# Idle products on the four quarters of the TensorE array in a kernel of linear attention and a mixture of experts

## The chip, the cores and the metric

The kernel runs on one core of one Trainium2 chip, in one launch. The metric is the device time of that launch in microseconds (us). Three runs before the change took 336.48, 336.76 and 333.15 us, median 336.48. PE is TensorE, PEld its loads of stationary operands, DVE is VectorE, ACT is ScalarE, POOL is GpSimd and SP is SyncE, which here only issues DMAs.

## The reference

A linear attention with 8 batches, 8 heads, 576 tokens and 64 columns feeds a soft mixture of 8 experts with 4 slots each. Cut to what is computed:

```
phi(x): p = x @ w_phi; p -= max|p| over the features; [exp(p), exp(-p)]      # 64 -> 2 x 128
kv = phi(k)^T v;  z = sum phi(k);  x = phi(q) kv / (phi(q) z + 1e-6)         # per batch and head
logits = x @ moe_phi                                                        # 4608 x 32 slots
d = softmax over tokens;  slots = d^T x                                     # 32 x 512
h = relu(slots @ w1[e]);  y = h @ w2[e]                                     # per expert, 512 -> 1024 -> 512
out = softmax over slots (logits) @ y                                       # 4608 x 512
```

## The kernel before

**Main loop.** The 64 pairs of batch and head are taken as 32 units of 1152 tokens. For each bank of four tiles of 128 tokens, `proj` (line 266) multiplies k and q by `w_phi` on the two halves of the array's rows, DVE takes maxima (lines 271 and 328), ACT takes exponentials (lines 297, 300, 333, 336), POOL weighs the values (line 286), and PE forms `kv` (`kvmm`, line 313, tile `kvp`) and the numerators (`num`, line 366, tile `psn`). Work of the mixture that can be done early (transposes `psx`, logits `psl`, slot sums `pss`) is put between.

**Close of the loop.** The last tokens' logits and the softmax over all tokens are finished (lines 514 to 616), in a chain of small steps between PE, DVE and ACT.

**The experts.** `layer1` (line 835, tile `hp`) and `layer2` (line 910, tile `yp`) multiply 32 columns at a time: four experts, or four chunks of the hidden layer, are put on the four quarters of the array's columns (`hp[...][32 * e:32 * e + 32]`, and `yp[q][g:g + 32]` with `g = 32 * (c % 4)`). Layer 2 runs in four quarters `q` of the output columns. When one is done, `slots` and `slots2` (lines 917 and 921, tiles `yt` and `psy`) sum it, and `outputs` (line 930, tile `pso`) multiplies the softmax over slots by it. DVE and ACT copy the result to `o` (line 934), and SP writes it out (line 935). The string `TAIL` sets the order of these steps.

**Weights.** The 64 tiles of the experts' weights (512 KB each, line 237) are read by SP in the second half of the kernel, as the buffers of the main loop are closed.

**Order.** The order of the main loop and of its close is written out in the string `ORDER`, one letter for each task. The tasks run on their engines in that order, and PE's whole program is one straight list of instructions without loops.

**Idle products.** `spin` (line 190) multiplies a 128 x 128 bf16 block by 512 columns, into a PSUM tile `psw` that nothing reads. It keeps PE at work while it would wait for others. There are 19 of these: `NWARM = 8` at the very start, while the first inputs come in; `NSPIN = 8` (letter `e`), six after the first two banks and one each after two of the first pieces of `kvmm`; and `NFIN = 3` (task `zspin`, letter `W`) in the close of the loop. In the program each is one load and one product.

A product of fp32 operands in the source stands in the trace as two loads and two products of its shape, and the counts below are those of the trace.

## Time and profile before

| | before |
|---|---|
| runs | 336.48, 336.76, 333.15 us |
| the profiled execution's own time | 332.36 us |
| its span, first to last instruction | 330.6 us |
| PE busy | 317.3 us (96%), 7094 products |
| PE's loads busy | 270.6 us (82%), 7094 loads |
| DVE, ACT, POOL busy | 239.7, 229.0, 160.9 us |
| read and written | 63.60 and 9.44 MB, 221 GB/s over the span |
| packets on the instruction queue of PE (q8) | 56, 0.92 MB |

The page names each group of instructions by line, engine, operation and tiles. The chain of waits follows the work that ended last back from the end: a piece named "issue" is time in which the engine at the end of the chain waited for nothing that the profile shows. A window is a stretch of the span, with each engine's busy time and, as xN, the instructions that ran in it, those included that were still running at its start. Two of the DMA queues, q8 and q14, carry instructions and not data.

### The profile page before, as it was taken

What the parts mean: (1) busy time and instruction counts of PE and PEld (TensorE: products, weight loads), DVE (VectorE), ACT (ScalarE), POOL (GpSimd) and SP (SyncE); (2) the same over time, 40 slices, a digit from 0 to 9 for tenths busy, and PEclk for the clock granted to TensorE, in tenths of its full rate; (3) what the DMA queues carried; (4) which work ended last, traced back from release to release, by engine and by line L of the source; (5) the groups of instructions that cost most, each with busy time, mean ns of one, the idle gap of its engine ahead of it and who ended that gap; (6) DMA issues with size and microseconds to landing.
All of it is one profiled execution on the core that took longest, in us unless ns stands there. A gap on an engine that the chain in (4) does not pass through costs nothing.

```text
span 330.6 us, 16700 instructions
## 1 busy us (share of the span) xinstructions
PE 317.3 (96%) x7094; PEld 270.6 (82%) x7094; DVE 239.7 (73%) x688; ACT 229.0 (69%) x674; POOL 160.9 (49%) x339
## 2 busy tenths in 40 slices
PE   8999999999999999999999999999999999998990
PEld 4899999999979999998799999987989864375640
DVE  1678888786879888778898877688869667423461
ACT  4899889878886997788688987867878361002450
POOL 2455676773547668642867687236767210200000
PEclk9999999999999999999999999999999999999996
DMA  7556376644755774574567846216533999997897
GB/s 253 163 162 206 107 230 216 227 175 125 283 169 171 237 279 189 172 234 130 162 205 239 288 146 227 95 36 239 171 109 97 378 404 342 412 410 288 322 392 279
DMA packets 23130, 74.12 MB, mean 224 GB/s; under 512 B 2576, under 2 KB 2960, under 8 KB 23056
## 3 DMA queue, kind: packets, MB, share of 16 engines
q1 hardware_dynamic: 22768, 72.65, 62.7%
q8 instruction: 56, 0.92, 1.1%
q10 hardware_dynamic: 288, 0.40, 0.4%
q14 instruction: 18, 0.15, 0.1%
HBM read 63.60 MB, written 9.44 MB: 221 GB/s over the span
## 4 chain that ended last, share of the span: by engine, by line
PE 88%; DVE 3%; issue 3%; POOL 2%; DMA 1%; ACT 0%; DVEq 0%; POOLq 0%; SPq 0%; ACTq 0%
PE kvp L313 22%; PE psn L366 20%; PE psk L266 11%; PE psq L266 11%; PE psx L719 5%; PE hp L835 4%; PE yp L910 4%; PE psl L423 3%; PE pso L930 2%; PE psw L190 2%; PE pss L455 1%; POOL vs L286 1%; DMA out<-o 1%; PE psd L448 1%; PE pss L570 1%
## 5 line engine op out<-in xcount | busy, mean ns | idle before, releaser
L286 POOL TENSOR_TENSOR vs<-vt,mk 128x520 f32<-128x520 f32 (+3 forms) x128 | 91.4, 730 | 64.2 <-ACT mk L275 45.5
L313 PE MATMUL kvp<-vs,kf 128*64 128x65 f32 (+1 forms) x2304 | 91.5, 229 | 0.4 <-POOL vs L286 0.3
L313 PEld LDWEIGHTS kvp<-vs,kf 128*64 128x64 f32 x2304 | 81.0, 138 | 6.7 <-POOL vs L286 1.8
L366 PE MATMUL psn<-kvs,qf 128*64 128x65 f32 x2304 | 79.9, 223 | 0.4 <-DVE un L382 0.3
L266 PE MATMUL psk<-wd,xs 64*128 64x128 f32 x576 | 76.3, 280 | 0.9 <-issue 0.7
L366 PEld LDWEIGHTS psn<-kvs,qf 128*64 128x64 f32 x2304 | 73.4, 138 | 3.4 <-issue 0.7
L266 PE MATMUL psq<-xs,wd 64*128 64x128 f32 x576 | 75.5, 280 | 0.0
L266 PEld LDWEIGHTS psk<-wd,xs 64*128 64x128 f32 x576 | 67.7, 187 | 4.2 <-issue 2.5
L266 PEld LDWEIGHTS psq<-xs,wd 64*128 64x128 f32 x576 | 67.3, 187 | 3.4 <-issue 1.1
L271 DVE TENSOR_REDUCE mk<-psk 128x4 f32<-128x512 f32 x72 | 48.5, 675 | 11.6 <-PE psk L266 6.7
L328 DVE TRANSPOSE_TENSOR_REDUCE mts<-psq 128x16 f32<-128x512 f32 x72 | 50.4, 705 | 8.1 <-PE psk L266 3.3
L297 ACT ACTIVATE kf<-psk 128x512 f32<-128x512 f32 x72 | 42.5, 591 | 16.7 <-DVE mk L271 5.1
L333 ACT ACTIVATE qf<-psq 128x512 f32<-128x512 f32 x72 | 42.2, 594 | 10.2 <-DVE dn L397 3.7
L412 POOL TENSOR_TENSOR xc<-un,dn 128x256 f32<-128x256 f32 x62 | 37.9, 614 | 17.5 <-DVE dn L397 14.3
L377 DVE TENSOR_TENSOR un<-psn,eq 128x195 f32<-128x195 f32 x96 | 33.0, 351 | 16.3 <-PE psn L366 7.7
L336 ACT ACTIVATE qf<-psq 128x512 f32<-128x512 f32 x72 | 43.0, 601 | 0.8 <-DVE mts L328 0.8
L300 ACT ACTIVATE kf<-psk 128x512 f32<-128x512 f32 x72 | 42.7, 596 | 0.1
L382 DVE TENSOR_TENSOR un<-psn,un 128x195 f32<-128x195 f32 x96 | 32.9, 350 | 1.1
L344 ACT ACTIVATE mh<-mts 32x36 f32<-32x36 f32 x128 | 29.5, 230 | 3.2 <-DVE mts L328 1.6
L350 DVE TENSOR_REDUCE eq<-mh 32x9 f32<-32x36 f32 x128 | 26.3, 205 | 1.5
L274 ACT ACTIVATE mk<-mk 128x4 f32<-128x4 f32 x72 | 15.1, 209 | 11.2 <-DVE mk L271 9.9
L934 DVE COPY o<-pso 128x384 f32<-128x384 f32 x24 | 12.1, 551 | 14.2 <-PE pso L930 14.2
(121 smaller groups left out, 313.3 us busy)
## 6 DMA issues: line engine op xcount, KB each, us to landing
wt<-w SPq DMA_DIRECT2D x64, 512.0 KB, 5.9
xs<-xT SPq DMA_DIRECT2D x36, 512.0 KB, 4.3
vt<-vv SPq DMA_DIRECT2D x31, 325.0 KB, 3.8
out<-o SPq DMA_DIRECT2D x24, 384.0 KB, 4.2
vt<-vv ACTq DMA_DIRECT2D x1, 325.0 KB, 3.5
xs<-xT SPq DMA_DIRECT2D x2, 128.0 KB, 3.3
cs<-cst SPq DMA_DIRECT2D x1, 128.0 KB, 3.0
wd<-w ACTq DMA_DIRECT2D x1, 64.0 KB, 1.8
```

Source lines behind the costliest of these rows:

```text
L266: nc.tensor.matmul(ps, l, r, start=True, stop=True)
L271: nc.vector.tensor_reduce(km[b][:, 2], kx[b], axis=AX, op=ALU.max, apply_absolute_value=True)
L286: nc.gpsimd.tensor_tensor(vs[b][:, :, place(b, u, t, o):place(b, u, t, o) + n], v[:, t + o:t + o + n].unsqueeze(1).broadcast_to([128, 2, n ...
L297: nc.scalar.activation(kf[b][:, 1], kx[b], AF.Exp, scale=-1.0)
L300: nc.scalar.activation(kf[b][:, 0], kx[b], AF.Exp)
L313: nc.tensor.matmul(ps[f:f + FE // 2, pn, o:o + m], kf[b][:, pn, NT * u + t - 4 * b, f:f + FE // 2], v2[:, pn, at:at + m], start=(t == 0 an ...
L328: nc.vector.tensor_reduce(mts.rearrange("p r j -> p j r")[:, o:o + 4], qx[b].rearrange("p j (r t) -> p (j r) t", t=32), axis=AX, op=ALU.ma ...
L333: nc.scalar.activation(qf[b][:, 0], qx[b], AF.Exp)
L336: nc.scalar.activation(qf[b][:, 1], qx[b], AF.Exp, scale=-1.0)
L366: nc.tensor.matmul(ps[64 * f:64 * f + 64, j, pn], q2[:, pn, 64 * f:64 * f + 64], kv[:, pn, b2], start=True, stop=True)
L377: nc.vector.tensor_tensor(un[u][:, CH * c:CH * c + CH], nx[s][:, :, 0], e[:, 1].unsqueeze(2).broadcast_to([128, CH, 65]), op=ALU.mult)
L412: divider(u).tensor_tensor(x[:, :, h * D:(h + 1) * D], un[u][:, a:b, 0:64], dn[u][:, a:b].unsqueeze(2).broadcast_to([128, b - a, 64]), op= ...
```

## The change

A second function, `spins`, does an idle product as eight: the four quarters of 32 columns of the same block, each by 256 columns, and this twice, into the two halves of the same PSUM tile. All thirteen idle products from the last two of the first eight on use it: two of `NWARM`, all eight of `NSPIN`, all three of `NFIN`. The first six stay as they were. Each of the thirteen is now 16 instructions and not 2, so PE's program is 13 x 14 = 182 instructions longer: 28 of these stand before the first `proj`, 84 in the six idle products after the first two banks, 28 in the two among the first pieces of `kvmm`, and 42 in the close of the loop. All 182 stand ahead of layer 1 and layer 2. No wait, no DMA and no other instruction is added, on PE or elsewhere, and nothing else changes its place.

```diff
     def spin(ps, x):
         nc.tensor.matmul(ps.rearrange("p (a c) -> p a c", c=128), x, x.unsqueeze(1).broadcast_to([128, 4, 128]), start=True, stop=True)
+
+    def spins(ps, x):
+        for j in range(8):
+            g = slice(32 * (j % 4), 32 * (j % 4) + 32)
+            nc.tensor.matmul(ps[g, 256 * (j // 4):256 * (j // 4) + 256].rearrange("p (a c) -> p a c", c=128), x[:, g], x.unsqueeze(1).broadcast_to([128, 2, 128]), start=True, stop=True)
+
     for i in range(NWARM):
-        spin(pmm.tile([128, 512], F32, tag="mm", name="psw"), warm)
+        (spin if i < NWARM - 2 else spins)(pmm.tile([128, 512], F32, tag="mm", name="psw"), warm)
...
-        add("spin", i, PE, 0.22 if i > 1 else 0.43, lambda: spin(bank3("spin", [128, 512], "psw"), warm), after=[("proj", 0)], get=["psn", ("nm", "spin")], put=["psn", ("nm", "spin")], lat=0.0, at=1e6)
+        add("spin", i, PE, 0.22 if i > 1 else 0.43, lambda: spins(bank3("spin", [128, 512], "psw"), warm), after=[("proj", 0)], get=["psn", ("nm", "spin")], put=["psn", ("nm", "spin")], lat=0.0, at=1e6)
...
-        add("zspin", i, PE, 0.22, lambda: spin(bank3("spin", [128, 512], "psw"), cs[:, 0:64].bitcast(mybir.dt.bfloat16)), at=1e6, after=[("num", NK - 1)], get=["psn", ("nm", "spin")], put=["psn", ("nm", "spin")], lat=0.0)
+        add("zspin", i, PE, 0.22, lambda: spins(bank3("spin", [128, 512], "psw"), cs[:, 0:64].bitcast(mybir.dt.bfloat16)), at=1e6, after=[("num", NK - 1)], get=["psn", ("nm", "spin")], put=["psn", ("nm", "spin")], lat=0.0)
```

PE's list in the close of the loop before, around the first of the three idle products there (`psl` are logits, `psd` a transpose, `cs` holds the identity):

```order
L531 MATMUL psl<-xT,phs 32x128 x4
L531 MATMUL psl<-xm,phs 32x128
L190 LDWEIGHTS cs
L190 MATMUL psw<-cs 128x512
L423 MATMUL psl<-xT,phs 32x128 x12
L448 MATMUL psd<-cs,eT 128x128
```

The same place now, from the same first row, cut after the fourth of the eight loads and products:

```order
L537 MATMUL psl<-xT,phs 32x128 x4
L537 MATMUL psl<-xm,phs 32x128
L195 LDWEIGHTS cs
L195 MATMUL psw<-cs 32x256
L195 LDWEIGHTS cs
L195 MATMUL psw<-cs 32x256
L195 LDWEIGHTS cs
L195 MATMUL psw<-cs 32x256
L195 LDWEIGHTS cs
L195 MATMUL psw<-cs 32x256
```

Four more such pairs follow, and then the logits as before: one load and one product became eight of each, and the neighbours stay.

PE's list in layer 2 before, from the sum of the first quarter on (each x4 of `yp` is eight products in the trace):

```order
L921 MATMUL psy<-yt,cs 128x128
L910 MATMUL yp<-wt_5808,sh 32x128 x4
L910 MATMUL yp<-wt_5925,sh 32x128 x4
L930 MATMUL pso<-ct,yt 128x384 x4
L910 MATMUL yp<-wt_5927,sh 32x128 x4
L910 MATMUL yp<-wt_5929,sh 32x128 x4
```

The same place now:

```order
L927 MATMUL psy<-yt,cs 128x128
L916 MATMUL yp<-wt_5878,sh 32x128 x4
L916 MATMUL yp<-wt_5995,sh 32x128 x4
L936 MATMUL pso<-ct,yt 128x384 x4
L916 MATMUL yp<-wt_5997,sh 32x128 x4
L916 MATMUL yp<-wt_5999,sh 32x128 x4
```

Here nothing moved but line and buffer numbers: each instruction stands 182 places further down in PE's program than before.

## The prediction

> **What bounds the kernel now.** I read the page first, then the waits of PE, then the chain of waits around the largest of them.

> ```profile
> PE 317.3 (96%) x7094; PEld 270.6 (82%) x7094; DVE 239.7 (73%) x688; ACT 229.0 (69%) x674; POOL 160.9 (49%) x339
> q8 instruction: 56, 0.92, 1.1%
> PE 88%; DVE 3%; issue 3%; POOL 2%; DMA 1%; ACT 0%; DVEq 0%; POOLq 0%; SPq 0%; ACTq 0%
> PE yp L910 <- issue: 1.4, 1, 1.4
> PE psk L266 <- issue: 0.7, 1, 0.7
> ```

> PE is busy 96% of the span and carries 88% of the chain, so what is put on PE's path, or taken off it, moves the end nearly one for one. Its largest waits in mid-kernel, 1.4 and 0.7 us, are for "issue": no engine and no data transfer released them. The queue q8 holds 56 packets, one for every 14,188 / 56 = 253 of PE's products and loads. So I read it as the queue that brings PE's own instructions, a block at a time. Here is the chain of waits in layers 1 and 2 (start, us, what):

> ```profile
> 287.52 3.57 PE hp L835 x32
> 291.09 1.31 PE yp L910 x48
> 292.40 1.02 PE psh L888 x8
> 293.42 3.63 PE yp L910 x128
> 297.05 0.42 PE psy L921 x2
> 297.47 0.56 PE yp L910 x12
> 298.03 1.44 issue
> 299.47 0.41 PE yp L910 x4
> 299.88 0.86 PE pso L930 x8
> 300.74 1.45 PE yp L910 x48
> ```

> PE stops in the middle of a row of equal products. Two things tie this stop to a block of instructions. The first is the DMA view: 291.50 to 296.95 holds packets of data (q1, first row) and one for another engine (q14), none of q8; 296.90 to 298.10 holds one (second row). The second is the distance to the other stop, at 245.37 (below): the window between them (last row) holds 883 products and 883 loads, 1766 in all, or seven times 252.

> ```profile
> q1 hardware_dynamic: 612, 2.23, 102.7%
> q8 instruction: 1, 0.02, 5.4%
> 246.08:298.04 51.96, 51.33 (x883) 34.57 (x883) 31.04 (x118) 18.72 (x55) 11.71 (x25) 1.00 0.85 329
> ```

> Both stops thus lie at the start of a block of about 126 products with their loads. Counting 126 products back from 298.03 (12 yp, 2 psy, 112 of the 128 yp at 3.63 / 128 = 0.0284 us) puts the start of the block before at 297.05 - 112 x 0.0284 = 293.87. If the next block is asked for when one is entered, its packet began 3.1 us after that, and the first product of it ran at 299.47, or 5.6 us after the request. Layer 2 goes through 126 products in about 4.2 us, so PE ran dry. [...]

> The other stop is in the main loop (timeline of PE):

> ```profile
> 240.44 1.83 PE L313 MATMUL kvp<-vs,kf 128*64 128x65 f32 x48
> 242.10 1.57 PE L366 MATMUL psn<-kvs,qf 128*64 128x65 f32 x48
> 243.50 0.64 PE L313 MATMUL kvp<-vs,kf 128*64 128x65 f32 x16
> 243.97 0.87 PE L366 MATMUL psn<-kvs,qf 128*64 128x65 f32 x24
> 246.10 0.37 PE L266 MATMUL psk<-wd,xs 64*128 64x128 f32 x1 [0.74 <-issue]
> ```

> Back from it, 5 products of `proj`, 24, 16, 48 and 33 of the 48 `kvp` make 126: the block before began at about 240.96, so the request took 5.1 us here and PE waited 0.74 us.

> **The change, part by part.** *The stop in layer 2.* The 182 instructions ahead of it move every block boundary 182 instructions, 91 products, to the front of the work. Back from 298.03 these are 12 yp, 2 psy and 77 yp: the boundary comes at 297.05 - 77 x 0.0284 = 294.87. The product at 298.03 is then in the middle of a block, and its 1.44 us go. The block entered at 294.87 ends 126 - 91 = 35 products behind the old stop: 4 yp, 8 pso, 23 of the 48 yp, at 300.74 + 23 x 0.0302 = 301.43, less the 1.44 us, 299.99. It lasts 5.1 us against the 5.6 of the request: a new stop of 0.5 us. The block before it starts 126 products back from 294.87 (51 yp, 8 psh, 48 yp, 19 of the 32 hp), at 291.09 - 19 x 0.112 = 288.97, and lasts 5.9 us: no stop. The request is bounded from below by no wait in the queue (the packet at once, and 299.47 - 296.95 = 2.5 us from packet to product), which leaves no stop, and from above by a packet that waits for the last weights:

> ```profile
> 297.00:299.00 2.00, 1.03 (x18) 0.64 (x14) 0.00 (x0) 0.27 (x1) 0.00 (x0) 1.00 0.99 387
> 299.00:301.00 2.00, 1.53 (x24) 0.79 (x28) 0.24 (x1) 0.20 (x1) 0.00 (x0) 1.00 0.64 252
> 313.00:315.00 2.00, 2.00 (x56) 1.26 (x48) 1.15 (x3) 0.99 (x4) 0.00 (x0) 1.00 0.55 208
> 315.00:317.00 2.00, 2.00 (x52) 1.26 (x48) 1.15 (x4) 0.95 (x4) 0.00 (x0) 1.00 1.03 404
> ```

> The DMA engines are full to 299 (share 0.99) and done with the weights soon after (0.64). A packet at 300.0 gives a product at 302.5, a stop of 2.5 us. I take 0.5, from the same place, 1.2 us on in the work. Net: -1.44 + 0.5 = -0.9, between -1.44 and +1.1. It reaches the end: until 315 the outputs don't fill the DMA engines (0.55), then they do (1.03), and a PE that is 0.9 us earlier starts that full stretch 0.9 us earlier.

> *The stop in the main loop.* Ahead of it stand 140 of the 182 (the last 42 are in the close), 70 products: the boundary moves to 70 products before 245.37 (5, 24, 16 and 25 of 48 psn), 242.77. The block that ends there:

> ```profile
> 237.60:242.75 5.14, 5.14 (x135) 4.95 (x132) 4.64 (x14) 4.34 (x13) 3.62 (x9) 1.00 0.49 162
> 126.02:130.06 4.04, 4.04 (x135) 4.00 (x131) 3.74 (x13) 3.87 (x12) 3.62 (x9) 1.00 0.82 323
> ```

> Its 5.14 us cover a request of 5.1; the next block, to the product that ran at 248.74, lasts as long without the 0.74. So -0.74, or -0.2 if the request takes layer 2's 5.6. The 45 or so other blocks of the main loop get new boundaries too. The shortest that I find, second row, has 4.04 us. The old block beside it saw its packet late, between 130.5 and 131.7:

> ```profile
> q8 instruction: 1, 0.02, 5.1%
> ```

> It was entered 70 products into the new one, at 126.02 + 70 / 126 x 4.04 = 128.3. So at least 2.2 us of queue and 2.5 behind it, 4.7, would stop the new block for 0.7 us. I take 0, since of all the main loop's old blocks one stopped PE visibly, and keep 0.7 for the range.

> *The idle products themselves.* The chain at both ends of the kernel:

> ```profile
> 0.94 3.46 PE psw L190 x8
> 4.39 1.89 PE psk L266 x15
> 6.28 1.40 PE psw L190 x6
> 7.68 0.13 issue
> 10.95 0.32 PE psw L190
> 12.56 0.32 PE psw L190
> 268.75 0.32 PE psw L190
> 270.48 0.32 PE psw L190
> 272.25 0.22 PE psw L190
> ```

> [...] Eight quarter products have four times 512 columns between them. Layer 1 and layer 2 show that products on the four quarters run side by side: 32 hp of 512 fp32 columns in 3.57 us are 0.446 for each four, and 128 yp are 0.113 for each four of 128 columns, 0.88 ns per column both times. A full-width bf16 product has 0.233 / 512 = 0.455 ns per column, so fp32 costs two passes, and quarters in bf16 should have 256 x 0.455 = 0.117 us for each four, twice, 0.233: the same as before. So 0, with -0.1 for each of the four at 0.32 (to the 0.22 of the last row) as the lower end, and for the upper end the loads. Four quarter loads of fp32 last 0.14 us in this trace:

> ```profile
> 299.47 0.14 PEld L910 LDWEIGHTS yp<-wt,sh 128*32 128x32 f32 x4 [1.71 <-issue]
> ```

> In line with the products, 2 x 0.14 = 0.28 each, 13 x 0.28 - 0.13 = +3.5 us. I take 0, since yp sets off a load and a product every 0.028 us, or eight in 0.227. [...]

> Sum: -0.9 - 0.74 + 0 = -1.7 us (rounded) on the profiled 332.36 (span 330.6 and 1.8 around it), or 330.7. The profiled execution lies below all three runs shown; against their median of 336.48 the same sum gives **334.8 us**.

> **The rivals.**
> - *The fetch is held to the end of the weights.* For it: 3.1 us of queue in layer 2 with the share at 0.99. Against: the packet of before did start in the full stretch. It decides from a packet at 298.4 on (an extra stop of 0.94). With the packet at 300.0 and the short block's 0.7: +1.1 - 0.74 + 0.7 = +1.1, slower than before, 337.6.
> - *The stops stay.* If they come at certain times, with the traffic, and not at certain instructions, they keep their 1.44 + 0.74 = 2.2 us: 336.5. Against: the distance of seven equal blocks. [...]
> - *All gains, no new stop, four shorter idle products.* -1.44 - 0.74 - 0.4 = -2.6: 333.9. [...]
> - *The quarters run one after another.* [...] Against it stand the hp and yp rows.
> - *The loads are not hidden*: +3.5 - 1.7, 338.3.
> [...]

> **How the numbers follow.** Chances: the forecast 0.55, fetch held 0.14, the stops stay 0.08, all gains 0.10, quarters in line 0.03, loads 0.05, clock 0.05. The three runs shown span 3.6 us, 1.1%, so 1% is about what can be told from no change. The range goes from the lowest run less the sum and less 0.4 for the idle products (333.15 - 2.1 = 331.0) to the held fetch, 337.6; it leaves out quarters, loads and clock (0.13) and a little at each end. Faster by over 1% (under 333.1): 0.11 from the forecast, if the runs lie at the low end of that spread, and 0.04 from all gains, 0.15. Slower by over 1% (over 339.8): quarters 0.03 and the upper ends of loads, clock and fetch 0.05, 0.08. Within 1%: 0.77.

> **What would show it.** After the change PE has no "issue" at the place of the old 1.44, and a shorter one some 35 products behind it, in the yp rows that follow the first eight pso. None stands where 5 `psk` and `psq` products had run at 245.37. Idle products show as x8 at 0.22 to 0.33 us together, and `psk` starts near 4.4. It would be wrong if a stop of over 1.4 us stands in layer 2, if psw grows to 0.5 us or more, or if the stops keep their places.

## The result, and the profile after

The changed kernel is slower: 337.16 us (median of 21 runs, 334.64 to 339.98) against 333.77 us (21 runs of the kernel before, 331.26 to 337.06), a ratio of 1.0105 with a 95% interval of 1.0083 to 1.0127. Two of the three runs that the prediction had (336.48 and 336.76) belong to a slower state that some runs fall into, over 1.5% above the kernel's fastest, so each ratio here is of the fast runs alone, and the times of the experiments below are medians of those. The profiled execution of the changed kernel took 335.14 us (span 333.4) against 332.36 (330.6), so the 2.8 us between the two traces stand for the 3.4 us between the medians.

The page after, with the same parts as before, and its PE waits of the kind "issue":

```profile
PE 318.3 (95%) x7185; PEld 272.2 (82%) x7185; DVE 239.8 (72%) x688; ACT 229.5 (69%) x674; POOL 161.4 (48%) x339
q8 instruction: 57, 0.93, 1.1%
PE 89%; DVE 3%; POOL 2%; issue 2%; ACT 1%; DVEq 0%; POOLq 0%; ACTq 0%
PE psn L372 <- issue: 2.5, 3, 1.1
PE kvp L319 <- issue: 0.8, 1, 0.8
PE yp L916 <- issue: 0.6, 1, 0.6
```

PE is busy 1.0 us longer (318.3 against 317.3). Both old waits are gone, 1.4 us in `yp` and 0.7 us in `psk`; in their place stand one of 0.6 us in `yp` and four in the main loop that had none there, 2.5 + 0.8 us. Layer 2 in the chain of waits after, from the sum of the first quarter on:

```profile
300.53 0.42 PE psy L927 x2
300.95 0.57 PE yp L916 x16
301.53 0.86 PE pso L936 x8
302.38 0.88 PE yp L916 x25
303.27 0.56 issue
303.83 0.86 PE yp L916 x23
```

The row that had been cut after 12 of 16 `yp` runs through, and the stop is now behind 25 of the 48 `yp` after the first `pso`. The main loop's new stops, from PE's timeline (start, us, what, the wait ahead of it):

```profile
54.29 1.32 PE L372 MATMUL psn<-kvs,qf 128*64 128x65 f32 x38 [0.36 <-issue]
69.39 0.50 PE L372 MATMUL psn<-kvs,qf 128*64 128x65 f32 x9 [1.02 <-issue]
129.49 0.62 PE L319 MATMUL kvp<-vs,kf 128*64 128x65 f32 x13 [0.80 <-issue]
134.90 1.32 PE L372 MATMUL psn<-kvs,qf 128*64 128x65 f32 x37 [1.09 <-issue]
```

Are these starts of blocks? The windows between the four stops and to the one in layer 2 hold 381 + 380, 1393 + 1393, 127 + 127 and 3664 + 3664 products and loads:

```profile
54.28:69.38 15.10, 14.08 (x381) 13.34 (x380) 11.36 (x33) 11.72 (x35) 9.91 (x21) 1.00 0.49 171
69.38:129.48 60.10, 59.23 (x1393) 54.31 (x1393) 48.77 (x132) 48.15 (x146) 35.78 (x74) 1.00 0.62 205
129.48:134.89 5.41, 4.31 (x127) 4.15 (x127) 4.01 (x12) 4.32 (x12) 3.94 (x9) 1.00 0.56 192
134.89:303.82 168.93, 167.50 (x3664) 140.75 (x3664) 127.15 (x391) 111.89 (x334) 81.34 (x171) 1.00 0.63 226
```

That is 761, 2786, 254 and 7328: 3, 11, 1 and 29 times 252 to 254. All five stand on one grid of blocks, the grid that the prediction placed. With PE's semaphore instructions counted too, which the windows leave out, the distances are 769, 2816, 256 and 7424 instructions: 3, 11, 1 and 29 times 256, to within one.

To see where the time goes, take each PE instruction's start after less the start of the same instruction before. This offset is flat, and changes only in steps:

| place before, us | step, us | what stands there |
|---|---|---|
| start | +0.17 | |
| 48.9, 53.7, 58.2 | +0.15, +0.54, +0.16 | new block starts |
| 67.4 | +1.26 | new block start |
| 126.4, 130.4 | +1.06, +1.36 | new block starts |
| 133.4 | -0.25 | block start of before |
| 246.5 | -1.11 | block start of before (its 0.74, and what followed it) |
| 256.8 | -0.15 | |
| 299.5 | -1.81 | block start of before (its 1.44, and a product's length) |
| 301.4 | +0.85 | new block start |

The main loop lost 4.53 us at six new block starts and won 1.36 at two old ones. Layer 2 won 0.96. With the start this makes 2.2 of the 2.5 us by which the last products are late; the rest is in steps too small for this list.

What happened at the second largest of them, 69.39, shows the mechanism. SP's timeline after:

```profile
61.71 0.33 SPq L171 DMA_DIRECT2D xs<-xT  x1
62.09 0.90 SPq L243 DMA_DIRECT2D wt<-w  x2
```

The DMA view of two windows, 64.10 to 67.10 (first queue row) and 67.10 to 69.40 (the other two):

```profile
q1 hardware_dynamic: 325, 1.19, 98.2%
q1 hardware_dynamic: 26, 0.05, 5.5%
q8 instruction: 1, 0.02, 2.8%
```

The same two windows by engine (PE, PEld, DVE, ACT, POOL, granted clock, DMA share, GB/s):

```profile
64.10:67.10 3.00, 3.00 (x99) 2.97 (x97) 2.61 (x9) 2.71 (x6) 1.57 (x4) 1.00 0.98 397
67.10:69.40 2.30, 1.28 (x45) 1.14 (x40) 1.17 (x4) 0.78 (x3) 1.17 (x4) 1.00 0.09 32
```

```profile
60.55 0.33 SPq L171 DMA_DIRECT2D xs<-xT  x1
```

and the block was entered at 65.28, 4.7 us behind that and not 2.4 as after. The windows of before around its packet:

```profile
65.28:66.38 1.10, 1.10 (x43) 1.10 (x41) 1.10 (x4) 0.40 (x2) 0.00 (x0) 1.00 0.82 335
66.38:67.40 1.02, 1.02 (x41) 1.02 (x38) 0.57 (x3) 0.77 (x3) 0.57 (x2) 1.00 0.08 24
```

The data ran out 1.1 us after the entry (share 0.82, then 0.08), the DMA view has the one q8 packet in the second window, and PE did not stop.

The same count over the traces of all fourteen kernels of this text gives nearly every block start a packet of q8 of its own. At each of the 44 waits of over 0.3 us that stand on such a start, the first product came 2.2 to 2.6 us behind the start of its packet, and the packet had begun 2.2 to 4.7 us after the block before was entered. What varies, and decides, is thus how late the packet begins, against how long the block lasts. In layer 2 the packet did not wait for the data to run out: before, it began between 296.90 and 298.10, about 3 us after the entry, and the DMA engines stayed full until 299 (share 0.99 from 297 on).

### The profile page after: what moved, and what is told of

It is laid out like the page before. It is cut to its first block, busy times and chain, and to the rows that moved or that the text cites. A ratio compares the mean times of both kernels' runs of the same rounds, so it can differ in the third digit from the quotient of the medians.

```text
span 333.4 us, 16882 instructions
## 1 busy us (share of the span) xinstructions
PE 318.3 (95%) x7185; PEld 272.2 (82%) x7185; DVE 239.8 (72%) x688; ACT 229.5 (69%) x674; POOL 161.4 (48%) x339
## 4 chain that ended last, share of the span: by engine, by line
PE 89%; DVE 3%; POOL 2%; issue 2%; ACT 1%; DVEq 0%; POOLq 0%; ACTq 0%
PE kvp L319 22%; PE psn L372 20%; PE psk L272 11%; PE psq L272 10%; PE yp L916 5%; PE psx L725 5%; PE hp L841 4%; PE pso L936 3%; PE psl L429 3%; PE pss L461 2%; POOL vs L292 1%; PE psd L454 1%; PE psw L190 1%; POOL xc L418 1%; PE psw L195 1%
## 5 line engine op out<-in xcount | busy, mean ns | idle before, releaser
L372 PE MATMUL psn<-kvs,qf 128*64 128x65 f32 x2304 | 81.1, 223 | 2.9 <-issue 2.5
L272 PEld LDWEIGHTS psk<-wd,xs 64*128 64x128 f32 x576 | 67.4, 187 | 2.6 <-issue 1.1
```

What stands on the lines that cost most here:

```text
L272: nc.tensor.matmul(ps, l, r, start=True, stop=True)
L372: nc.tensor.matmul(ps[64 * f:64 * f + 64, j, pn], q2[:, pn, 64 * f:64 * f + 64], kv[:, pn, b2], start=True, stop=True)
```

## Experiments

Theory A: the quartered products cost nothing; the place of the block starts against the bursts of loads costs. Theory B: the quartered products, or their loads, cost. Each ratio is to the kernel before on the same chip, with its 95% interval. "Steps" are of the offset described above, each from one traced execution.

**Same places, no quartered product.** In the changed kernel:

```diff
     def spins(ps, x):
-        for j in range(8):
-            g = slice(32 * (j % 4), 32 * (j % 4) + 32)
-            nc.tensor.matmul(ps[g, ...], x[:, g], ..., start=True, stop=True)
+        spin(ps, x)
+        for j in range(14):
+            nc.tensor.ldweights(x[:, 32 * (j % 4):32 * (j % 4) + 32], tile_position=(0, 32 * (j % 4)))
```

> All thirteen idle products are full-width again, each followed by 14 bare weight loads of 32 columns, so that every other instruction of PE stands exactly where it stands in the changed kernel, with no quartered product left. The loads themselves may cost something next to the idle products (15 loads at about 0.03 us against a product of 0.23 us: up to 0.2 us each, 2.6 us in all, within the first 13 us and the close). If it is the place of the block boundaries that costs: the main loop stops at the changed kernel's boundaries (near 54, 69, 128 and 133 us, together 3.5 to 5 us), the stops of before at 133 and 245 us and the 1.44 us in layer 2 are gone, a stop of 0.3 to 1.2 us stands in the yp rows that follow the first eight pso, and the ratio is 1.006 to 1.018. If the quartered products cost: no new stop over 0.3 us in the main loop, and a ratio of 0.993 to 1.004.

339.69 us against 333.34, ratio 1.0206 (1.0125 to 1.0287): slower even than the changed kernel, without one quartered product. PE's timeline, its stops of over 0.25 us for "issue":

```profile
56.07 1.32 PE L372 MATMUL psn<-kvs,qf 128*64 128x65 f32 x37 [0.46 <-issue]
70.92 0.46 PE L372 MATMUL psn<-kvs,qf 128*64 128x65 f32 x9 [0.99 <-issue]
94.90 0.37 PE L272 MATMUL psk<-wd,xs 64*128 64x128 f32 x1 [0.66 <-issue]
133.03 0.51 PE L319 MATMUL kvp<-vs,kf 128*64 128x65 f32 x11 [1.75 <-issue]
137.56 1.50 PE L372 MATMUL psn<-kvs,qf 128*64 128x65 f32 x45 [0.27 <-issue]
177.23 0.51 PE L372 MATMUL psn<-kvs,qf 128*64 128x65 f32 x10 [0.78 <-issue]
308.44 0.85 PE L916 MATMUL yp<-wt,sh 128*32 128x128 f32 x21 [0.46 <-issue]
```

The same products are cut as after (`psn`, `psn` x9, `kvp`, `psn`, and `yp` in layer 2). Two more of the same grid came in, at 94.9 and 177.2 (and one of 0.21 us at 197.5), and the sum of the new steps is about 7 us, above the 3.5 to 5 expected. So is the ratio, above the 1.006 to 1.018. This execution is some 1.5 us later than the changed kernel's from the first banks on, and that is its bare loads: in the chain of waits each of the six idle products there takes 0.48 us with its fourteen loads, against 0.233 before. That this moved block entries against the transfers is a guess. What does not hold is that the quartered products cost: there are none here, and the stops stand where they stood. Loads of 32 columns are still here, so of their part in B the next run decides.

**Quarters, the old places.** The first eight idle products are quartered too, two of `NSPIN` are made of 16 products of 128 columns, the close is left as before: 256 more instructions, exactly one block, ahead of the main loop and of layer 2.

```diff
-        (spin if i < NWARM - 2 else spins)(pmm.tile([128, 512], F32, tag="mm", name="psw"), warm)
+        spins(pmm.tile([128, 512], F32, tag="mm", name="psw"), warm)
...
-lambda: spins(bank3("spin", [128, 512], "psw"), warm)
+lambda i=i: spins(bank3("spin", [128, 512], "psw"), warm, 4 if i in (2, 3) else 2)
```

> The quarters stay, but their number is chosen so that 256 instructions, one whole block, stand ahead of the main loop instead of 140: all first eight idle products are done as eight quarters, two of the next ones as sixteen quarters of 128 columns, and the three in the close of the loop are full-width again. Theory A (the time goes to the places at which PE crosses from one block of instructions to the next): the boundaries fall where they fell before the change, the stops of the main loop at 68, 128 and 133 us go, the ones of before at 245 and 298 come back, and the ratio to before is 0.998 to 1.003. Theory B (products on quarters cost time by themselves, wherever the boundaries fall): the ratio stays at 1.008 to 1.013.

334.08 against 333.07, ratio 1.0025 (0.9989 to 1.0062). No new step of 0.3 us or more in the main loop, and both old stops are back at their products:

```profile
247.00 0.37 PE L273 MATMUL psk<-wd,xs 64*128 64x128 f32 x1 [0.80 <-issue]
300.69 0.41 PE L917 MATMUL yp<-wt,sh 128*32 128x128 f32 x4 [1.77 <-issue]
```

With sixteen quartered products, their loads and the old grid, the time is that of before within the interval. The two runs together leave the grid.

**One part alone.** The ten early products quartered (140 instructions ahead of everything from the main loop on), and the three of the close alone (42 ahead of layer 2):

```diff
-lambda: spins(bank3("spin", [128, 512], "psw"), cs[:, 0:64]...
+lambda: spin(bank3("spin", [128, 512], "psw"), cs[:, 0:64]...
```

This is the edit for the ten; for the three, the other two lines of the change are put back in the same way.

> Only the ten early idle products are quartered: 140 instructions more ahead of the main loop, and 140 instead of 182 ahead of the experts. Theory A: the main loop is that of the changed kernel, with its stops of about 4.5 us against 0.9 before; in layer 2 a boundary after 140 instructions makes a stop of about 0.9 us instead of 1.44; ratio 1.008 to 1.014. Theory B: ten thirteenths of the loss, ratio 1.006 to 1.010. What tells them apart is the place: by A the two kernels' products keep a constant distance between block boundaries and lose it only at them.

336.74, ratio 1.0117 (1.0056 to 1.0178). The main loop has the changed kernel's stops (steps +0.82, +1.79, +1.69, +1.09; `psn` x38, `psn` x9, `kvp` x13, `psn` x45), and the stops of before are gone there too. Its main loop is the changed kernel's, instruction for instruction, and still the stop at `psn` x9 is 1.54 us here and 1.02 there, and the one at `kvp` 1.42 and 0.80: single stops of one main loop differ by some 0.5 us between executions. In layer 2 the new stop stands one block later than I had expected it:

```profile
306.80 0.41 PE L916 MATMUL yp<-wt,sh 128*32 128x128 f32 x2 [1.17 <-issue]
```

> Only the three idle products in the close of the loop are quartered: 42 instructions more ahead of the experts, none in the main loop. Theory A: the main loop is that of before; in layer 2 the block that ends there lasts about 4.0 us instead of 4.2, so its stop grows from 1.4 to about 1.6 us; ratio 0.998 to 1.003. Theory B: three thirteenths of the loss, ratio 1.002 to 1.004.

332.29, ratio 0.9954 (0.9918 to 0.9991): faster than both kernels, by little over the noise where before is concerned. The main loop keeps its old grid, and in layer 2 the wait is 0.68 us instead of 1.44. I had expected 1.6 there: I had let the packet wait until the burst ended, but it came 2.4 us after the entry.

```profile
300.13 0.42 PE L916 MATMUL yp<-wt,sh 128*32 128x128 f32 x7 [0.68 <-issue]
```

**The gain in layer 2 alone.** In the kernel before, 182 bare loads of 32 columns are put between the first 48 products of layer 1, behind the main loop:

```diff
                                      start=kc == 0, stop=kc == KC - 1, skip_group_check=True)
+                    for _ in range(pads.pop(0) if pads else 0):
+                        nc.tensor.ldweights(cs[:, 0:16].bitcast(mybir.dt.bfloat16), tile_position=(0, 32 * e))
```

> The kernel before with its full-width idle products, and 182 loads of 32 columns (with no product of their own) spread over the first three quarters of layer 1, four behind each product: the 182 instructions without any quarter of an idle product and without a shift in the main loop. Theory A: the main loop is that of before, and layer 2 has the short stop of the changed kernel, 0.5 us instead of 1.44: -0.9 us, ratio 0.996 to 0.999 if the loads hide behind the products, and slower by what they don't hide, up to 182 x 0.028 = 5 us, all of it in layer 1. Theory B: no quarters, no loss, and no gain in layer 2 either: a stop of 1.44 us there.

332.19, ratio 0.9963 (0.9930 to 0.9997), with the changed kernel's layer 2:

```profile
300.24 0.86 PE L914 MATMUL yp<-wt,sh 128*32 128x128 f32 x23 [0.57 <-issue]
```

The stop stands ahead of the same 23 `yp` with the same length, 0.57 against 0.56, and the steps in layer 2 are the same (-1.81, +0.86). The loads themselves, 2.7 us on the load path, lie hidden under layer 1. So the moved grid is worth in layer 2 what it was predicted to be, about 1 us in this trace. The ratio can't be put down to it alone: in this execution the stop at 245 is gone as well (a step of -1.03; the packet began 1.5 us after the entry and not 2.8), though nothing ahead of it was changed.

**Fewer bursts.** Are the waits for a packet made by the data? First, 30 of the 32 loads of `v` are left out, of before and of the changed kernel (the first two tiles are used again, so the values of `v` are not those of the reference):

```diff
     def vload(u):
+        if u > 1:
+            vt[u] = vt[u % 2]
+            return
```

> The kernel before, with 30 of its 32 loads of values (325 KB each) left out: from the third unit on the values of the first two are used again, so the output is another one, and 9.75 MB less are read; PE's program is the same instruction for instruction. The data comes in shorter bursts. Theory A1 (a block of instructions waits behind the data that is queued when it is asked for): the stops in the main loop of before, 0.3 and 0.7 us, go or shrink, layer 2 keeps its 1.4 us; ratio 0.994 to 1.000. Theory A2 (a block takes about 5 us to come at these places whatever the data does): nothing changes, 0.998 to 1.002.

> The changed kernel, with the same 30 loads of values left out. Theory A1: its stops in the main loop, about 4.5 us in all, shrink to under 1.5 us, packets there start within 2 us of the request instead of 2.7 to 3.7, layer 2 keeps its 0.6 us; ratio to the kernel before 0.993 to 1.000, no slower than the kernel before with the same loads left out by more than 0.3%. Theory A2: the stops stay, ratio 1.007 to 1.012.

332.84 and 335.69 against 333.72: ratios 0.9989 (0.9956 to 1.0023) and 1.0069 (1.0035 to 1.0102). In the first the stop at 245 is gone, which proves little, as it was gone once with all the loads too, and two steps of 0.34 and 0.74 us are new. The second was a miss: I had expected under 1.5 us of new stops in the main loop, and the steps there sum to 3.85 us. The largest is at `psn` x9 again, 1.31 us: its burst is one of `xs` and weights, and they were still there. So I left out the weights' loads in the main loop too (28 of 30; the tiles of the first two are used again):

```diff
             i = len(wt)
+            if 1 < i < nslot[0]:
+                wt.append(wt[i % 2])
+                continue
```

> The kernel before with 30 of 32 loads of values and 28 of the 30 loads of weights that stand in the main loop left out (earlier tiles are used again, so the output is another one): what is left in the main loop are single 512 KB loads of inputs, 1.3 us of traffic each. PE's program is the same. Theory A1 (a block of instructions waits until the burst of data that is queued at its request has drained): no stop over 0.3 us in the main loop; the weights of layer 2 still come in one long stretch, and its 1.4 us stays. Ratio 0.994 to 1.000. Theory A2 (blocks are slow at certain places whatever the data does): 0.998 to 1.002.

> The changed kernel with the same 30 loads of values and 28 loads of weights left out. Theory A1: its 4.5 us of stops in the main loop fall to under 0.6 us in all, packets there start within 1.6 us of the request; layer 2 keeps its short stop of 0.6 us; so it is now faster than the kernel before, ratio 0.990 to 0.999, and 0.5 to 1 us under the kernel before with the same loads left out. Theory A2: the stops stay, ratio 1.006 to 1.012.

The window from 10 to 250 us of the kernel before:

```profile
10.00:250.00 240.00, 238.80 (x5816) 220.97 (x5814) 195.61 (x546) 196.23 (x585) 146.83 (x306) 1.00 0.56 184
```

The changed kernel:

```profile
10.00:250.00 240.00, 236.25 (x5741) 218.20 (x5742) 192.79 (x538) 194.84 (x582) 146.09 (x302) 1.00 0.55 184
```

Before, with few loads:

```profile
10.00:250.00 240.00, 239.49 (x5829) 221.74 (x5827) 196.53 (x548) 197.29 (x587) 148.33 (x306) 1.00 0.27 81
```

The changed kernel, with few loads:

```profile
10.00:250.00 240.00, 239.35 (x5847) 221.63 (x5844) 196.58 (x548) 197.01 (x587) 148.01 (x308) 1.00 0.26 81
```

In these 240 us PE is idle 1.2 us before and 3.75 after. At under half the traffic (81 GB/s) it is 0.5 and 0.65: the changed grid costs next to nothing where the bursts are gone. Is that more than two executions of one program differ by? In the other kernels with all the loads, PE is idle 0.7 to 1.3 us with the main loop of before (the 256 instructions, the close alone, the loads in layer 1) and 4.9 us with that of the changed kernel (the ten early products alone). So the fall from 3.75 to 0.65 is clear, and that from 1.2 to 0.5 is not. The whole times, 337.45 and 337.41 against 333.23 (1.0131, 1.0092 to 1.0169, and 1.0135, 1.0089 to 1.0181), missed what was expected and say nothing on this: tiles used again held back the weights of the experts, whose last loads SP sent out at about 301 us and not 292, and the end came later for it, which I had not thought of. Only the main loop compares.

**Bursts spread.** If the bursts are the cause, smaller ones might be a cure. SP's order is changed so that 27 of the 30 loads of weights in the main loop stand one load of inputs earlier (letter `x` in `ORDER`); PE's list is unchanged. A piece of it:

```diff
-...fktharujnovmvkbdicnogpcjdwmgwflrjhirqvaw"
-"mxfysbkrkdtnomlhizvnoc...
+...fktharujnovmvkxbdicnogpcjdwmgwflrjhirqvaw"
+"mfysbkrkdtnomlhizvnoc...
```

> The changed kernel with the same loads and the same program of PE; SP issues 27 of the main loop's 30 loads of weights one load of inputs earlier, so that a load of weights no longer stands in the queue behind a load of inputs that just started, with two of them never behind one. Theory A1 (a block waits for the burst that is queued at its request): the longest bursts shrink from 1.5 to about 1 MB, the stops in the main loop fall from 4.5 us to 1 to 2.5 us and lie at other boundaries; layer 2 as in the changed kernel. Ratio to before 1.000 to 1.006. If the bursts' order does not matter: 1.008 to 1.012.

> Quarters only in the three idle products of the close (42 instructions, main loop as before), and the loads of weights issued one load of inputs earlier as in the other run. Theory A1: stops in the main loop 0 to 0.8 us against 1.0 before, layer 2 with 0.7 us against 1.44; ratio 0.992 to 0.999. If the order of loads does not matter: 0.994 to 0.997, as with the three quarters alone.

Misses both. The changed kernel with it: 336.88 against 332.98, ratio 1.0101 (1.0065 to 1.0138), no better than without. The kernel quartered in the close alone lost what it had won, 0.9998 (0.9966 to 1.0030). PE's timeline of the first:

```profile
69.32 0.50 PE L356 MATMUL psn<-kvs,qf 128*64 128x65 f32 x9 [1.86 <-issue]
129.10 0.62 PE L303 MATMUL kvp<-vs,kf 128*64 128x65 f32 x14 [0.47 <-issue]
135.60 0.57 PE L356 MATMUL psn<-kvs,qf 128*64 128x65 f32 x13 [2.25 <-issue]
```

The block that runs out ahead of 135.60 was entered at 129.10. Two windows of this kernel:

```profile
129.10:133.30 4.20, 4.20 (x127) 4.15 (x127) 3.40 (x12) 3.93 (x12) 2.96 (x7) 1.00 0.81 297
133.30:135.60 2.30, 0.05 (x2) 0.00 (x0) 0.63 (x2) 0.76 (x3) 1.20 (x2) 1.00 0.03 7
```

The q8 packet lies in the second, from 133.34 on, 4.2 us after the entry, when the data is through (0.81, then 0.03). In this order the bursts sit elsewhere, and they are no smaller. With the same list on PE, the stop at `psn` x9 went from 1.02 to 1.86 us and the one behind `kvp` from 1.09 to 2.25, while the one at `kvp` fell from 0.80 to 0.47. Differences of some 0.5 us come with the execution, as the ten early products showed; the 2.25, behind a packet that began 4.2 us after the entry, is beyond them, so there the order of the loads very likely set the price.

**Another grid.** 28 instructions ahead of the main loop and 70 ahead of layer 2 (two of `NSPIN` and the close quartered), which by laying the new starts over the old trace's bursts looked free:

```diff
-        (spin if i < NWARM - 2 else spins)(pmm.tile([128, 512], F32, tag="mm", name="psw"), warm)
+        spin(pmm.tile([128, 512], F32, tag="mm", name="psw"), warm)
...
-lambda: spins(bank3("spin", [128, 512], "psw"), warm)
+lambda i=i: (spins if i < 2 else spin)(bank3("spin", [128, 512], "psw"), warm)
```

> Quarters in two of the idle products after the first banks (28 instructions) and in the three of the close (42): 28 more ahead of the main loop, 70 ahead of layer 2. Theory A, with the waits of the blocks of the trace of before laid over the new boundaries: no stop of over 0.3 us in the main loop, the 0.74 us at 245 gone; in layer 2 the block from 291.8 us on lasts 4.4 us, a stop of 0.6 to 1.2 us instead of 1.44. Ratio 0.993 to 0.999. By theory B (quarters cost by themselves) five thirteenths of the loss, 1.004.

335.82, ratio 1.0060 (1.0022 to 1.0098), a miss: five new steps in the main loop (0.36, 0.48, 0.41, 0.58, 1.11 us), 2.9 us in all. So I could not say from one trace which grid is free. What stays open is why: this execution was 2.4 us later by the end of the first banks than the trace that I had laid under it, and each stop moves what follows, but neither was varied by itself.

## Why the prediction was wrong

The forecast was 334.8 us, 1.7 below the median shown; measured was 337.16, 3.4 above the median of the 21 runs of before.

- *Blocks of about 126 products with their loads, a request on entry.* Held: the stops of two programs lie on two grids, 182 instructions apart in layer 2; the distances after are 3, 11, 1 and 29 times 256 with PE's semaphore instructions counted; and nearly every block start has its own packet (56 before, 57 after). That the request is made on entry is read from this; no view shows the request itself.
- *The stop in layer 2: -1.44 + 0.5 = -0.9.* Held, in place (predicted 23 `yp` into their row of 48, found after 25) and size (0.56 new, -0.96 net; the same in the trace with the bare loads in layer 1).
- *The stop at 245: -0.74.* Held in the two traces compared, and worth 1.11 with what followed it. As a term for the median it was too large: with the same main loop the wait was 0.74, 0.80 and 0.47 us in three traces and none in a fourth (the loads in layer 1).
- *The idle products: 0.* Held to 0.2 us. The chain of waits after, at the start and at two single ones:

```profile
0.94 2.74 PE psw L190 x6
3.68 0.97 PE psw L195 x12
4.65 1.16 PE psk L272 x11
11.10 0.33 PE psw L195 x8
12.72 0.33 PE psw L195 x8
```

Eight quarters take 0.33 us where one product took 0.32. The six behind the first banks took 1.40 / 6 = 0.233 us each before, the figure that the forecast's 0 starts from. The two at the start take 0.97 where two took 0.86, and `psk` starts at 4.65 and not at 4.39, which is within what starts differ by. The eight loads for each of them cost nothing here that shows, as the `yp` rows had said.
- *The other blocks of the main loop: "I take 0, since of all the main loop's old blocks one stopped PE visibly, and keep 0.7 for the range".* **This is the step that failed.** It measured +4.53 us, at six of some 45 blocks. The block named there, 126 to 130, did end in a stop, as that paragraph worked out (a step of 1.36 us against 0.7), and so did the one before it (1.06). The working was at hand and was not carried through to the other blocks: 5.6 us from entry to product had been seen in layer 2, 5.1 in the main loop, and a block of the main loop lasts about 60.1 / 11 = 5.5 us (the window after from 69.38 to 129.48). With so little between, whether a block is followed by a stop depends on how late the next packet begins (2.2 to 4.7 us after the entry at the 44 waits). That the old grid had stopped for 0.74 and 0.25 us only was the luck of that grid, no property of the main loop: another grid measured new steps of 2.9 us (28 instructions ahead), and the changed kernel's own grid 5.8 and about 7 us in two other kernels (the ten early products alone, the bare loads). What sets the wait of a packet at a given place, and so the price of a grid ahead of time, stays open.
- *The rival on the slow side* had the kind of mechanism that decided, a packet held by data (in 240 us of the changed kernel PE is idle 3.75 us with all the loads and 0.65 with few), but put it in layer 2 alone with 0.7 for the main loop. Its 337.6 lies near 337.16 for another reason than it gave.
- *The clock,* 0.05 in the chances. No run shows a clock that rises later with quarters: in the traces before and after, PE's granted clock reads 1.00 from 0.94 to 4.39 us, where an idle product took 3.46 / 8 = 0.43 us before, and 1.00 from 6.28 to 7.68, where one took 0.233. At 15 us the traces with quarters among the first idle products lie 0.2 to 2.4 us behind that of before, and those without 0.2 to 2.3 (the bare loads left aside), so the quarters don't show in it.
- *The median.* The median of the three runs shown lay 2.7 us above that of the 21, in which they are counted; with 333.77 the same sum would have given 332.1, and the miss would have been 5 us, not 2.4.

Of the 57 blocks of the trace after, 50 show no new stop; the other seven cost 4.53 + 0.56 = 5.1 of its 335 us.

## What to carry to other kernels

In the straight program of this kernel, added instructions moved every block start behind them (182 of them moved the grid in layer 2 by 182), and that alone was worth -0.5% to +1.2%. So compare such an edit against one of the same length that does nothing, or pad to a whole block of 256, before a time is put down to the edit itself. Where a profile shows "issue" on a busy engine at multiples of about 253 of its instructions, look at what transfers were sent out just before the block was entered: a burst of 1.5 MB lasts about 4 us at the 397 GB/s seen here, and at the two block starts of the main loop looked at above the next block's packet came when it was through, 3.0 and 4.2 us after the entry.

## What the runs showed that I had not expected

- At the two block starts of the main loop looked at above, the instruction packet began when the data already queued had run out: after 3.0 us in the changed kernel (325 packets of q1 in that time, 20 for each of 16 engines on average), after 4.2 us with the loads in another order. In layer 2 it began after about 3 us amid the data (before: share 0.99 from 297 to 299, packet at 296.99). What decides when it begins, no run here tells.
- Bare loads of 32 columns are nearly free under layer 1: 182 of them took 95 ns each on the load path,

```profile
L839 PEld LDWEIGHTS <-cs 128*32 128x32 bf16 x182 | 2.7, 95 | 2.8 <-issue 2.8
```

and the kernel with them is 0.37% faster than without. It and the kernel with the close alone quartered (0.9954) are the versions that beat both kernels, by intervals that end just under 1 (0.9997 and 0.9991). In both traces the shorter stop in layer 2 is what their block starts win, and an edit ahead of layer 2 can undo that.
- One program's executions differ by up to 2.3 us in their first 10 us. In the kernel with the close alone quartered, which changes nothing there, the chain of waits has

```profile
4.53 3.02 PE psk L272 x16
7.56 2.62 PE psw L190 x6
```

where the trace of before had 1.89 us for 15 products and 1.40 us for the same six. Six in 2.62 us are 0.44 each, near the price of the very first ones of before (0.43) and not the 0.233 of the same six there. What follows came 2.3 us later.
